# Split weights decoded from float64: three bitwise VectorE instructions behind a ScalarE scaling, and the low part made by an adding transfer

## The chip, the cores and the metric

The kernel runs on one core of a Trainium2 chip. The metric is the device time of one execution in microseconds (us); the median of three runs of the kernel before is 1067.02 us.

## The reference

Linear attention with random features, and behind it a two-layer feed-forward network whose activation is `h - tanh(h)`. There are 4608 tokens (8 batches of 576), 8 heads of 64, 128 features, a model width of 512 and an inner width of 2048.

```python
def phi(x):                                  # x: q or k, scaled by D**-0.25
    h = einsum('bhsd,md->bhsm', x, omega) - sum(x*x)/2
    return exp(h - max(h)) / sqrt(m)
q_p, k_p = phi(q), phi(k)
kv, z = einsum('bhsm,bhsd->bhmd', k_p, v), sum(k_p, axis=2)
x = (q_p @ kv) / (q_p . z + 1e-6)            # (4608, 512) after a transpose
h = x @ w_in                                 # w_in  (512, 2048), float64
out = (h - tanh(h)) @ w_out                  # w_out (2048, 512), float64
```

The two weight matrices are float64. The chip multiplies float32 and the reduced float32r, so the kernel turns each weight into a sum of two float32r numbers, a high and a low part, and multiplies with both.

## The kernel before, in words

**Weights.** The inner width is cut into 16 slices `f` of 128. One load, `fetch(f)`, brings slice `f` of both matrices as `raw[f]`: 128 partitions with 1024 float64 words, 1 MB. `decode(f)` makes `wt[f]` of it, which has the same size and lies in the same place: `wt[f][:, 0]` is the high part and `wt[f][:, 1]` the low part, 1024 numbers per partition each. The work tiles of a decode are `a` (the value being built, 4 KB per partition, two buffers) and `m` (the low bits, one buffer). ScalarE takes the absolute value of the upper half-words (L438) and copies a 16-bit piece from the middle of the words (L440). A clamp follows (L442), on VectorE for the first two slices and on GpSimd for the other 14. VectorE shifts and masks (L444), joins the sign (L445) and builds the low bits (L448). ScalarE rounds the result to the high part (L452, written `w<-a`), and VectorE isolates the exponent (L453) and multiplies the low bits by it (L454).

**Attention.** `k_unit(b, c)` handles batch `b` and head pair `c`: a load `kf`, features on TensorE into `pj`, exponentials on ScalarE (`phi_k`, L164), and the sums `pk`, from which `kvf` and `zb` are copied. GpSimd lays the last 64 tokens out in `kd` and `vd` (L184, L185). `q_unit(ch, c)` handles a chunk of 256 tokens: `qf`, `pj_q`, `phi_q`, denominators `dn` on VectorE (L347, L350), a scaling by them (L355 on ScalarE, L357 on VectorE), transposes `pt`, a copy `qt` (L369) and the product `pn` (L374). The quotient is split into `xh` and `xl`.

**Feed-forward.** Chunks 0 and 1 go through together, in 16 steps of one slice each: `h_0_s` is the first product (12 matmuls of 512 columns, L471), then tanh on ScalarE (`g`, L475), `g = h - g` on VectorE (L476), the rounding `gh` on ScalarE (L477), the rest `gl` on VectorE (L478), and 12 matmuls into four output banks (L489 to L491). There are two banks for `h`, so `h_0_2` starts when VectorE has read `h_0_0`. Chunks 2 to 17 follow, in eight steps of two slices each, with the later attention units between them; they use the weights that are on the chip by then.

**Order.** A Python generator per unit and a clock `t` set the program's order. The weights are decoded between attention units: slice `f` not before beat 4 + 2.5 `f`. A scheduler then orders each engine's instructions by its own estimate of time, and each engine carries its list out strictly in that order. Loads are issued by SyncE, in program order at first. The pool `a0` holds what only the first three chunks need; slices 10 to 15 take its place when it is closed, so their loads start only then.

Of the kernel before, what the change touches and what calls it, by code (L numbers as in the profile page):

```python
# [8 lines left out]
F32 = mybir.dt.float32  # L9
F32R = mybir.dt.float32r  # L10
U64 = mybir.dt.uint64
U32 = mybir.dt.uint32
U16 = mybir.dt.uint16
AF = mybir.ActivationFunctionType
ALU = mybir.AluOpType
AX = mybir.AxisListType
# [2 lines left out]
NT, DM, DFF = B * S, H * D, 2048  # L19
P = 128  # L20
# [5 lines left out]
E = D + 2  # L26
SCALE = float(D) ** -0.25
EPS = 1e-6 * M


@with_exitstack
def favor_attention_ffn(ctx: ExitStack, tc: tile.TileContext, qT, kT, va, vt, omT, w, out):
# [12 lines left out]
    nc = tc.nc  # L45
# [8 lines left out]
    def open_pool(name, side="right"):  # L54
        pools[name] = tc.tile_pool(name=name, bufs=1, side=side, reuse_waits="tile")
        return pools[name].__enter__()
# [7 lines left out]
    def bank(kind):  # L64
        tags = mode[kind]
        tags.append(tags.pop(0))
        return tags[-1]
# [26 lines left out]
    dec = open_pool("dec")  # L94
# [221 lines left out]
    def q_unit(ch, c):  # L316
# [23 lines left out]
        for h in range(2):  # L340
            for t in range(2):
                i = ix(h, t)
                for b, s, e in pieces:
                    s, e = max(s, t * P), min(e, (t + 1) * P)
                    if s < e:
                        r = slice(s - t * P, e - t * P)
                        nc.vector.tensor_tensor_reduce(  # L347
                            bank("junk")[r], ph[r, i], kvs[b, c][1][r, h], scale=1.0, scalar=EPS,
                            op0=ALU.mult, op1=ALU.add, accum_out=dn[r, i : i + 1])
# [63 lines left out]
    wt = {}  # L413

    raws = {}
# [11 lines left out]
    def decode(f):  # L427


        top = raws[f].bitcast(U32)[:, 1::2]  # L430
        topf = raws[f].bitcast(F32)[:, 1::2]
        mid = raws[f].bitcast(U16)[:, 1::4]
        a = dec.tile([P, 2 * DM], U32, tag="a", name=f"a{f}", bufs=2)
        m = dec.tile([P, 2 * DM], U32, tag="m", name=f"m{f}", bufs=1)

        nc.scalar.activation(a.bitcast(F32), topf, AF.Abs)  # L438

        nc.scalar.activation(m, mid, AF.Copy, scale=128.0)  # L440
        engine = nc.vector if f < 2 else nc.gpsimd
        engine.tensor_scalar(a.bitcast(F32), a.bitcast(F32), 2.0**-15, 122879.9921875,  # L442
                             op0=ALU.max, op1=ALU.min)
        nc.vector.tensor_scalar(a, a, 3, 0x3FFFF000, op0=ALU.logical_shift_left, op1=ALU.bitwise_and)  # L444
        nc.vector.scalar_tensor_tensor(out=a, in0=top, scalar=0xC0000000, in1=a,  # L445
                                       op0=ALU.bitwise_and, op1=ALU.bitwise_or)

        nc.vector.scalar_tensor_tensor(out=m, in0=top, scalar=23, in1=m,  # L448
                                       op0=ALU.logical_shift_left, op1=ALU.bitwise_or)

        wt[f] = places[f].tile([P, 2, 2 * DM], F32R, tag=f"w{f}", name=f"w{f}")
        nc.scalar.copy(wt[f][:, 0], a.bitcast(F32))  # L452
        nc.vector.tensor_scalar(a, a, 0xFF800000, None, op0=ALU.bitwise_and)  # L453
        nc.vector.scalar_tensor_tensor(out=wt[f][:, 1], in0=m, scalar=2.0**-43, in1=a.bitcast(F32),  # L454
                                       op0=ALU.mult, op1=ALU.mult)

    xh, xl = [sb.tile([P, 2, NC, TC], F32R, name=f"x{k}") for k in "hl"]

# [94 lines left out]
    while decoded < NF:  # L555
        if t in (2, 4):
            fetch(int(t == 4))
        if not gens and not start and len(places) < NF:
            close_pool("a0")
            weight_places(open_pool("w1", "left"), range(10, NF))  # L560
            for f in range(decoded, decoded + 2):
                fetch(f)
        if decoded in raws and t >= 4 + 2.5 * min(decoded, 16) + 2 * max(0, decoded - 16):
            decode(decoded)
            decoded += 1
            fetch(decoded + 2 - 1)
        if t == 15:
            mode.update(pj=["pj0", "pj1", "po1"], pk=["pk"], pt=["pt", "po0"])
        if done + 2 < decoded and t >= 23 + 1 * done:
            if done == 0:  # L570
                assert xdone[0] == xdone[1] == NC
                out_tiles(0, ("po0", "po1", "pj1", "pt"))
                mode.update(pj=["pj0"], pk=["pk"], pt=["pk"])
            step(done)
            done += 1
        tick(start.pop(t, ()))
        t += 1
# [89 lines left out]
```

## Time and profile before

| what | value |
|---|---|
| median of 3 runs | 1067.02 us (1065.73 to 1067.55) |
| profiled execution, from the first to the last instruction | 1065.4 us; no time of its own is given beside this span, and the median lies 1.6 us above it |
| TensorE busy | 1041.8 us, 98% |
| VectorE busy | 855.5 us, 80% |
| ScalarE busy | 696.4 us, 65% |
| GpSimd busy | 325.9 us, 31% |
| granted TensorE clock, mean | 0.998 |

The shares are means over the whole execution. Decoding lies in its first 160 us alone, where the engines stand otherwise than in the mean; a view of that stretch says more than the table. A row of the form `L440 ACT ACTIVATE m<-raw ... x16 | 18.7, 1166 | 9.7 <-DVE w L454` reads: line 440, ScalarE, what it writes and reads, 16 instructions of 1166 ns on average, and 9.7 us in which the engine was idle ahead of them, waiting for VectorE's L454.

### The profile page before, as it was taken

To read this page: it belongs to the slowest core of one execution; us is meant where nothing else is said; L and a number is where in the kernel's file an instruction comes from. 1 tells how busy PE (TensorE), PEld (TensorE's weight loads), DVE (VectorE), ACT (ScalarE), POOL (GpSimd) and SP (SyncE) were. 2 spreads that over 40 slices of the span, in tenths; PEclk is the share of its full clock that TensorE was granted. 3 is DMA by queue.
4 is the path that set the end of the run, shared out by engine and by line. 5 is a ranking of instruction groups with operands and counts; after the bars stand their busy time and mean duration, and the time that the engine had idled before them with its cause. 6 is when DMAs were issued, how large, how long until landed. Compare 5 with 4: busy or idle time off the path is not lost.

```text
span 1065.4 us, 20130 instructions
## 1 busy us (share of the span) xinstructions
PE 1041.8 (98%) x6760; PEld 945.6 (89%) x6760; DVE 855.5 (80%) x2910; ACT 696.4 (65%) x1773; POOL 325.9 (31%) x553
## 2 busy tenths in 40 slices
PE   7988999999999999999999999999999999999998
PEld 7766888999889999999999998999999999999997
DVE  5999995889998886789889878998888887666522
ACT  6997655777677665577777766677767675555422
POOL 4634541344333420133333344333333331000000
PEclk9999999999999999999999999999999999999999
DMA  8750401111111110011111111111101110000000
GB/s 265 237 213 3 187 1 42 53 39 46 31 53 33 54 33 31 11 53 33 53 34 53 34 37 44 33 53 29 47 25 49 33 37 11 30 16 21 1 21 21
DMA packets 35528, 55.90 MB, mean 52 GB/s; under 512 B 12256, under 2 KB 21600, under 8 KB 33376
## 3 DMA queue, kind: packets, MB, share of 16 engines
q1 hardware_dynamic: 35344, 54.57, 16.3%
q8 instruction: 54, 0.88, 0.3%
q14 instruction: 50, 0.41, 0.1%
q10 hardware_dynamic: 80, 0.03, 0.0%
HBM read 45.15 MB, written 9.44 MB: 51 GB/s over the span
## 4 chain that ended last, share of the span: by engine, by line
PE 61%; DVE 2%; ACT 1%; POOL 1%; issue 0%; DVEq 0%; POOLq 0%
PE h L471 26%; PE po L489 8%; PE po L490 8%; PE po L491 8%; PE pj_q L142 2%; PE pk L266 2%; PE pt L366 2%; PE pn L397 1%; PE pn L396 1%; PE pj_kb L142 1%; PE pj_ka L142 1%; PE pk L304 0%; PE pk L302 0%; DVE junk L347 0%; POOL khl L250 0%
## 5 line engine op out<-in xcount | busy, mean ns | idle before, releaser
L471 PE MATMUL h<-xh,w 128*128 128x256 f32 (+1 forms) x2176 | 450.1, 290 | 3.9 <-DVE g L476 2.1
L471 PEld LDWEIGHTS h<-xh,w 128*128 128x128 f32 x2176 | 354.8, 190 | 14.7 <-DVE g L476 3.2
L471 PE MATMUL h<-xl,w 128*128 128x256 f32 (+1 forms) x1088 | 315.8, 290 | 0.0
L489 PE MATMUL po<-w,gh 128*128 128x512 f32 x544 | 213.7, 393 | 0.0
L490 PE MATMUL po<-w,gh 128*128 128x512 f32 x544 | 213.3, 392 | 0.0
L471 PEld LDWEIGHTS h<-xl,w 128*128 128x128 f32 x1088 | 206.9, 190 | 6.0
L491 PE MATMUL po<-w,gl 128*128 128x512 f32 x544 | 209.2, 391 | 0.0
L477 ACT CAST gh<-g 128x512 fp32r<-128x512 f32 x144 | 89.4, 621 | 92.8 <-DVE g L476 91.3
L475 ACT ACTIVATE g<-h 128x512 f32<-128x512 f32 x144 | 85.4, 593 | 95.0 <-PE h L471 82.7
L476 DVE TENSOR_TENSOR g<-h,g 128x512 f32<-128x512 f32 x144 | 98.7, 686 | 57.8 <-ACT g L475 56.6
L478 DVE TENSOR_TENSOR gl<-g,gh 128x512 fp32r<-128x512 f32 x144 | 108.2, 751 | 34.9 <-ACT gh L477 33.1
L491 PEld LDWEIGHTS po<-w,gl 128*128 128x128 f32 x544 | 102.1, 188 | 20.5
L489 PEld LDWEIGHTS po<-w,gh 128*128 128x128 f32 x544 | 102.5, 188 | 16.2
L490 PEld LDWEIGHTS po<-w,gh 128*128 128x128 f32 x544 | 102.5, 188 | 15.3
L347 DVE CUSTOM_DVE_ANT_0 junk<-phi_q,zb 128x128 f32<-128x128 f32 (+1 forms) x320 | 98.5, 309 | 14.4 <-ACT phi_q L150 0.5
L150 ACT ACTIVATE phi_q<-phi_q,nb_q 128x128 f32<-128x128 f32 x240 | 79.6, 392 | 6.8 <-DVE nb_q L146 6.7
L442 POOL TENSOR_SCALAR a<-a 128x1024 f32<-128x1024 f32 x14 | 58.7, 4194 | 54.6 <-ACT a L438 37.2
L250 POOL TENSOR_TENSOR khl<-phi_ka,khl 128x256 fp32r<-128x256 f32 x48 | 37.9, 796 | 121.6 <-DVE khl L249 92.5
L258 POOL CAST vhl<-v 128x128 fp32r<-128x128 f32 (+1 forms) x144 | 45.8, 319 | 91.9 <-PE pk L266 71.5
L390 DVE TENSOR_TENSOR ql<-pt,qh 128x512 fp32r<-128x512 f32 x60 | 41.1, 685 | 32.3 <-ACT qh L389 31.8
L146 DVE CUSTOM_DVE_ANT_0 phi_q<-pj_q,phi_q 128x128 f32<-128x128 f32 x240 | 56.0, 283 | 2.3 <-ACT phi_q L143 2.2
L389 ACT CAST qh<-pt 128x512 fp32r<-128x512 f32 x60 | 34.9, 581 | 32.9 <-PE pt L366 32.6
(152 smaller groups left out, 1938.2 us busy)
## 6 DMA issues: line engine op xcount, KB each, us to landing
raw<-w SPq DMA_DIRECT2D x16, 1024.0 KB, 7.3
kf<-kT SPq DMA_DIRECT2D x32, 288.0 KB, 2.9
qf<-qT SPq DMA_DIRECT2D x72, 128.0 KB, 2.1
out<-o SPq DMA_DIRECT2D x36, 256.0 KB, 2.0
v<-vt SPq DMA_DIRECT2D x24, 288.0 KB, 2.8
v<-va SPq DMA_DIRECT2D x8, 288.0 KB, 5.9
omf<-omT ACTq DMA_DIRECT2D x1, 32.0 KB, 2.2
omf<-omT SPq DMA_DIRECT2D x1, 32.0 KB, 2.4
```

The costliest lines, as they stand in the source:

```text
L146: nc.vector.tensor_tensor_reduce(ph[:, j], pj[:, i, :M], ph[:, j], scale=-SCALE, scalar=3.0e38, op0=ALU.add, op1=ALU.min, accum_out=nb[:, ...
L150: nc.scalar.activation(ph[:, j], ph[:, j], AF.Exp, bias=nb[:, j : j + 1], scale=-1.0)
L347: nc.vector.tensor_tensor_reduce(bank("junk")[r], ph[r, i], kvs[b, c][1][r, h], scale=1.0, scalar=EPS, op0=ALU.mult, op1=ALU.add, accum_ou ...
L442: engine.tensor_scalar(a.bitcast(F32), a.bitcast(F32), 2.0**-15, 122879.9921875, op0=ALU.max, op1=ALU.min)
L471: nc.tensor.matmul(o, w_, x, start=i == 0, stop=i == len(prods) - 1)
L475: nc.scalar.activation(g, p, AF.Tanh)
L476: nc.vector.tensor_sub(g, p, g)
L477: nc.scalar.copy(gh, g)
L478: nc.vector.tensor_sub(gl, g, gh.bitcast(F32))
L489: nc.tensor.matmul(po[t], h, wt[f][:, 0, DM:], start=first, stop=False)
L490: nc.tensor.matmul(po[t], h, wt[f][:, 1, DM:], start=False, stop=False)
L491: nc.tensor.matmul(po[t], l, wt[f][:, 0, DM:], start=False, stop=last)
```

## The change: what it does

`decode(f)` builds the whole float32 value first. ScalarE scales the upper half-words by 2**-112 (L435 of the changed kernel), the clamp becomes a symmetric one (L437), VectorE shifts left by 3 (L438), joins the upper three bits of the lower half-word (L439) and the sign (L441). ScalarE then writes the rounded high part (L445) and, with a second instruction, its negative into the place of the low part (L446). A transfer issued by GpSimd adds the full value to that (L447): full value minus high part is the low part. The tile `m` is gone, and `a` has three buffers.

```diff
-        top = raws[f].bitcast(U32)[:, 1::2]
+        low, top = (raws[f].bitcast(U32)[:, i::2] for i in range(2))
         topf = raws[f].bitcast(F32)[:, 1::2]
-        mid = raws[f].bitcast(U16)[:, 1::4]
-        a = dec.tile([P, 2 * DM], U32, tag="a", name=f"a{f}", bufs=2)
-        m = dec.tile([P, 2 * DM], U32, tag="m", name=f"m{f}", bufs=1)
-        nc.scalar.activation(a.bitcast(F32), topf, AF.Abs)
-        nc.scalar.activation(m, mid, AF.Copy, scale=128.0)
+        a = dec.tile([P, 2 * DM], U32, tag="a", name=f"a{f}", bufs=3)
+        af = a.bitcast(F32)
+        nc.scalar.activation(af, topf, AF.Copy, scale=2.0**-112)
         engine = nc.vector if f < 2 else nc.gpsimd
-        engine.tensor_scalar(a.bitcast(F32), a.bitcast(F32), 2.0**-15, 122879.9921875,
-                             op0=ALU.max, op1=ALU.min)
-        nc.vector.tensor_scalar(a, a, 3, 0x3FFFF000, op0=ALU.logical_shift_left, op1=ALU.bitwise_and)
-        nc.vector.scalar_tensor_tensor(out=a, in0=top, scalar=0xC0000000, in1=a,
+        engine.tensor_scalar(af, af, -TOP, TOP, op0=ALU.max, op1=ALU.min)
+        nc.vector.tensor_scalar(a, a, 3, None, op0=ALU.logical_shift_left)
+        nc.vector.scalar_tensor_tensor(out=a, in0=low, scalar=29, in1=a,
+                                       op0=ALU.logical_shift_right, op1=ALU.bitwise_or)
+        nc.vector.scalar_tensor_tensor(out=a, in0=top, scalar=0x80000000, in1=a,
                                        op0=ALU.bitwise_and, op1=ALU.bitwise_or)
-        nc.vector.scalar_tensor_tensor(out=m, in0=top, scalar=23, in1=m,
-                                       op0=ALU.logical_shift_left, op1=ALU.bitwise_or)
         wt[f] = places[f].tile([P, 2, 2 * DM], F32R, tag=f"w{f}", name=f"w{f}")
-        nc.scalar.copy(wt[f][:, 0], a.bitcast(F32))
-        nc.vector.tensor_scalar(a, a, 0xFF800000, None, op0=ALU.bitwise_and)
-        nc.vector.scalar_tensor_tensor(out=wt[f][:, 1], in0=m, scalar=2.0**-43, in1=a.bitcast(F32),
-                                       op0=ALU.mult, op1=ALU.mult)
+        nc.scalar.copy(wt[f][:, 0], af)
+        nc.scalar.activation(wt[f][:, 1], af, AF.Copy, scale=-1.0)
+        nc.gpsimd.dma_start(wt[f][:, 1], af, accum_op=ALU.add)
```

Since the scheduler orders by its own estimates, the change also moves instructions that it does not name. Behind the decoding, lines of the changed kernel have numbers that are 10 lower (L465 for the tanh of L475). SyncE's list of loads is the same in both. Three places follow; names end in the buffer's number.

ScalarE before, around the tanh of step 0 (`g_0_0`) and its rounding (`gh_0_0`):

```order
L440 ACTIVATE m6_976<-raw6_746 128x1024
L438 ACTIVATE a7_1072<-raw7_908 128x1024
L355 ACTIVATE phi_q2_1_935<-phi_q2_1_935,dn_2_1_945 128x128 x2
L218 COPY kvf13_117<-pk_1_3_961 128x64 x2
L381 COPY x2_0_927<-pn_2_0_922 128x256
L475 ACTIVATE g_0_0_1110<-h_0_0_1097 128x512
L452 CAST w6_983<-a6_975 128x1024
L355 ACTIVATE phi_q2_2_1008<-phi_q2_2_1008,dn_2_2_1018 128x128 x2
L369 COPY qt_2_1_971<-pt_2_1_966 128x512
L224 COPY zb_1_3_1032<-pk_1_3_961 128x256
L477 CAST gh_0_0_1111<-g_0_0_1110 128x512
```

The same place of the changed kernel:

```order
L369 COPY qt_2_0_872<-pt_2_0_867 128x512
L355 ACTIVATE phi_q2_2_994<-phi_q2_2_994,dn_2_2_1004 128x128 x2
L218 COPY kvf13_117<-pk_1_3_949 128x64 x2
L369 COPY qt_2_1_959<-pt_2_1_954 128x512
L381 COPY x2_0_915<-pn_2_0_910 128x256
L465 ACTIVATE g_0_0_1094<-h_0_0_1081 128x512
L224 COPY zb_1_3_1018<-pk_1_3_949 128x256
L369 COPY qt_2_2_1025<-pt_2_2_1020 128x512
L445 CAST w9_1225<-a9_1219 128x1024
L446 ACTIVATE w9_1225<-a9_1219 128x1024
L467 CAST gh_0_0_1095<-g_0_0_1094 128x512
```

Before, the tanh of step 0 stands behind the ScalarE work of 21 decode instructions (eight of L438, seven of L440, six of L452); now behind that of 28 (ten scalings, nine roundings, nine negatives), and behind `phi_q2_2` and `qt_2_1` as well. On VectorE it is 32 decode instructions ahead of step 0's L476 (L466 now) where it was 35, all ten of the first slices instead of about seven. The two ScalarE instructions of slice 9 now stand between the tanh and `gh_0_0`, where those of slice 6 stood.

GpSimd before, from the last layouts to the clamp of slice 9:

```order
L442 TENSOR_SCALAR a4_734<-a4_734 128x1024
L184 COPY kd1_126<-kf_1_3_799 64x64 x2
L185 COPY vd1_127<-v1_125 64x66 x2
L442 TENSOR_SCALAR a5_896<-a5_896 128x1024
L442 TENSOR_SCALAR a6_975<-a6_975 128x1024
L442 TENSOR_SCALAR a7_1072<-a7_1072 128x1024
L442 TENSOR_SCALAR a8_1127<-a8_1127 128x1024
L442 TENSOR_SCALAR a9_1237<-a9_1237 128x1024
```

The same place of the changed kernel, where `DMA w<-a` is the issue of the adding transfer:

```order
L437 TENSOR_SCALAR a5_886<-a5_886 128x1024
L184 COPY kd1_126<-kf_1_3_789 64x64 x2
L185 COPY vd1_127<-v1_125 64x66 x2
L447 DMA w4_732<-a4_726 128x1024
L447 DMA w5_892<-a5_886 128x1024
L437 TENSOR_SCALAR a6_963<-a6_963 128x1024
L437 TENSOR_SCALAR a7_1058<-a7_1058 128x1024
L437 TENSOR_SCALAR a8_1111<-a8_1111 128x1024
L447 DMA w6_969<-a6_963 128x1024
L447 DMA w7_1064<-a7_1058 128x1024
L437 TENSOR_SCALAR a9_1219<-a9_1219 128x1024
```

Three clamps now run in a row ahead of the transfer of slice 6, and two issues stand ahead of the clamp of slice 9. The scaling of slice 9 on ScalarE writes the buffer of `a` that slice 6 used, so it waits until that transfer has landed.

TensorE before, at the end of step 2 (`h_0_2`) and behind it:

```order
L471 MATMUL h_0_2_1173<-xh_100,w2_447 128x512 x2
L471 MATMUL h_0_2_1173<-xl_101,w2_447 128x512
L471 MATMUL h_0_2_1173<-xh_100,w2_447 128x512
L374 MATMUL pn_2_1_1001<-qt_2_1_971,kvf01_107 128x64 x2
L374 MATMUL pn_2_1_1001<-qt_2_1_971,kvf11_115 128x192 x2
L366 MATMUL pt_2_2_1034<-ident_64,phi_q2_2_1008 128x128 x4
L489 MATMUL po1_0_1094<-w0_219,gh_0_0_1111 128x512
```

The changed kernel at the beginning of its step 2:

```order
L221 MATMUL pk_1_3_949<-ident_64,z_1_3_980 128x128 x2
L366 MATMUL pt_2_2_1020<-ident_64,phi_q2_2_994 128x128 x4
L374 MATMUL pn_2_1_987<-qt_2_1_959,kvf01_107 128x64 x2
L374 MATMUL pn_2_1_987<-qt_2_1_959,kvf11_115 128x192 x2
L461 MATMUL h_0_2_1155<-xh_100,w2_441 128x512
L461 MATMUL h_0_2_1155<-xl_101,w2_441 128x512
```

The transposes `pt_2_2` and the product `pn_2_1` stood behind `h_0_2` and stand ahead of it now; all other work ahead of `h_0_2` is the same.

2 lines of the change are left out of this document (1 added, 1 removed).

## The prediction

> **What bounds the kernel now.** Over the whole execution TensorE is busy 98% of the time. The change touches only the decoding, so the first view is the busy time by stretch, cut where the stretches differ (the columns are: length, then busy time and instructions of each engine):
>
> ```profile
> core 0: us, PE busy (x) PEld busy (x) DVE busy (x) ACT busy (x) POOL busy (x), PEclk, DMA share, GB/s
> 12.50:30.00 17.50, 14.15 (x78) 11.88 (x77) 15.03 (x29) 13.74 (x37) 8.46 (x9) 0.90 0.89 282
> 30.00:60.00 30.00, 28.11 (x161) 23.20 (x161) 30.00 (x91) 29.64 (x88) 13.57 (x19) 1.00 0.76 242
> 60.00:87.75 27.75, 21.95 (x118) 17.46 (x117) 27.39 (x102) 23.26 (x71) 8.97 (x3) 1.00 0.37 142
> 87.75:98.00 10.25, 8.12 (x47) 6.72 (x45) 10.02 (x22) 7.52 (x14) 7.79 (x2) 1.00 0.00 0
> 98.00:165.00 67.00, 67.00 (x299) 55.26 (x300) 59.66 (x75) 42.62 (x58) 31.35 (x10) 1.00 0.20 78
> ```
>
> From 98 us on TensorE is never idle, though six slices are still to be decoded: there a faster decode buys nothing. Between 30 and 87.75 us VectorE is full, and ScalarE nearly so: 0.36 us idle, then 4.49. TensorE idles 13.17 us in all from 12.5 to 98 us. That is everything the change could give back. Second view, what TensorE waited for from 20 to 98 us (the longest three):
>
> ```profile
> PE pn L374 <- ACT qt L369: 3.3, 4, 1.5
> PE pk L201 <- ACT phi_k L164: 2.5, 2, 2.0
> PE h L471 <- DVE g L476: 2.1, 2, 1.1
> ```
>
> It mostly waited for ScalarE; VectorE's two waits belong to steps 1 and 2. So ScalarE decides the stage, and the third view is ScalarE's own groups from 12.5 to 87.75 us, with what it waited for:
>
> ```profile
> L438 ACT ACTIVATE a<-raw 128x1024 f32<-128x1024 f32 x8 | 9.3, 1165 | 0.0
> L440 ACT ACTIVATE m<-raw 128x1024 uint32<-128x1024 uint16 x7 | 8.3, 1179 | 3.8 <-DVE w L454 3.8
> L355 ACT ACTIVATE phi_q<-phi_q,dn 128x128 f32<-128x128 f32 x20 | 7.8, 483 | 0.9 <-DVE dn L350 0.9
> L452 ACT CAST w<-a 128x1024 fp32r<-128x1024 f32 x6 | 6.6, 1101 | 0.1
> L214 ACT CAST kvw<-pk 128x128 fp32r<-128x128 f32 x4 | 1.4, 352 | 1.9 <-DVE z L210 1.9
> ```
>
> Of 8.61 us idle, VectorE caused 3.8 + 0.9 + 1.9 = 6.6 us.
>
> **What a decode costs.** VectorE's part by the rows of the first 200 us, and GpSimd's clamp:
>
> ```profile
> L448 DVE SCALAR_TENSOR_TENSOR m<-raw,m 128x1024 uint32<-128x1024 uint32 x16 | 20.4, 1272 | 0.1
> L445 DVE SCALAR_TENSOR_TENSOR a<-raw,a 128x1024 uint32<-128x1024 uint32 x16 | 20.3, 1269 | 0.0
> L454 DVE SCALAR_TENSOR_TENSOR w<-m,a 128x1024 fp32r<-128x1024 uint32 x16 | 19.5, 1217 | 0.1
> L453 DVE TENSOR_SCALAR a<-a 128x1024 uint32<-128x1024 uint32 x16 | 11.3, 703 | 4.1 <-ACT w L452 4.1
> L444 DVE TENSOR_SCALAR a<-a 128x1024 uint32<-128x1024 uint32 x16 | 11.0, 688 | 0.1
> L442 POOL TENSOR_SCALAR a<-a 128x1024 f32<-128x1024 f32 x14 | 58.7, 4194 | 54.6 <-ACT a L438 37.2
> ```
>
> VectorE: 0.688 + 1.269 + 1.272 + 0.703 + 1.217 = 5.15 us a slice before. Now one shift (0.688, at most L453's 0.703) and two joins of L445's shape (1.269 to 1.272): 3.23 us. It saves 1.92 us a slice, 30.7 us in all, 11.5 of them (six slices) behind 98 us, where TensorE covers them. ScalarE: 1.165 + 1.179 + 1.101 before. The scaling has the shape of L438. The negative has the shape of L452; its cost lies between 1.10 and L438's 1.17, and I take L452's, since shape and types are equal. That is 3.37 against 3.45: nothing gained worth counting. The clamp stays at 4.19 us.
>
> **What is added.** Sixteen issues on GpSimd and 16 transfers of 512 KB from SBUF to SBUF. Nearest rows, sizes with landing time, and an issue on SyncE's queue:
>
> ```profile
> raw<-w SPq DMA_DIRECT2D x16, 1024.0 KB, 7.3
> kf<-kT SPq DMA_DIRECT2D x32, 288.0 KB, 2.9
> 44.57 0.43 SPq L81 DMA_DIRECT2D raw<-w  x1
> ```
>
> An issue costs from 0.43 us (SyncE's) to 4.2 us (a clamp over the whole tile); I take 1.0 us, near the lower end because no elements pass through GpSimd. Sixteen are 16 us of GpSimd time; GpSimd idles 35 us between 30 and 87.75 us and 36 us from 98 to 165 us. Landing: between `kf` and `raw` a line gives 2.9 + (512 - 288) / 736 x 4.4 = 4.24 us; the ends are 2.9 us, `kf`'s own, and, since the target is read as well, 8.5 us, twice the line. I take 4.24. The Trainium skill ("DMA: Bandwidth & Descriptors", Anatomy of one DMA) fits a transfer issued from GpSimd by 2.0 us plus bytes over 436 GB/s; an estimate from that page is 3.2 us, and with it the wait of step 3 below, 0.5 us, would be gone and the sum 1066.3 us. The loads lose some of their engines' time (share 0.76 between 30 and 60 us); no TensorE wait of note ends on a load there, so I count nothing, and put its failure into the last rival.
>
> **The path that sets the end.** The relief goes to VectorE, but the order spends it: ahead of the tanh of step 0 stand ten slices' bitwise work instead of about seven, 32 decode instructions against 35, so VectorE is still full. ScalarE has 28 decode instructions there against 21. Its own rows around that tanh, and TensorE's around steps 2 and 3:
>
> ```profile
> 84.62 1.14 ACT L440 ACTIVATE m<-raw 128x1024 uint32<-128x1024 uint16 x1 [1.40 <-DVE w L454]
> 85.66 1.13 ACT L438 ACTIVATE a<-raw 128x1024 f32<-128x1024 f32 x1
> ...
> 87.75 0.59 ACT L475 ACTIVATE g<-h 128x512 f32<-128x512 f32 x1
> 88.23 1.04 ACT L452 CAST w<-a 128x1024 fp32r<-128x1024 f32 x1
> 89.17 0.70 ACT L355 ACTIVATE phi_q<-phi_q,dn 128x128 f32<-128x128 f32 x2
> 89.76 0.58 ACT L369 COPY qt<-pt 128x512 f32<-128x512 f32 x1
> 90.23 0.38 ACT L224 COPY zb<-pk 128x256 f32<-128x256 f32 x1
> 90.49 0.64 ACT L477 CAST gh<-g 128x512 fp32r<-128x512 f32 x1
> ```
>
> ```profile
> 89.82 0.50 PE L471 MATMUL h<-xh,w 128*128 128x512 f32 x1 [1.06 <-DVE g L476]
> ...
> 92.68 1.26 PE L374 MATMUL pn<-qt,kvf 128*128 128x64 f32 x8
> 93.78 0.60 PE L366 MATMUL pt<-ident,phi_q 128*128 128x128 f32 x4
> 94.14 0.47 PE L489 MATMUL po<-w,gh 128*128 128x512 f32 x1
> ...
> 97.93 0.50 PE L471 MATMUL h<-xh,w 128*128 128x512 f32 x1 [1.07 <-DVE g L476]
> ```
>
> From start to start a decode instruction takes 1.04 us (84.62 to 85.66) or 0.94 (88.23 to 89.17). The sum, step by step:
>
> 1. Seven more of them, at 1.04: +7.3 us. The two L355 of `phi_q2_2` (89.17 to 89.76) and the copy `qt_2_1` (89.76 to 90.23): +1.1 us.
> 2. All 6.6 us that ScalarE waited for VectorE come back: -6.6 us. The 2.0 us left wait for TensorE or stand at the start.
> 3. A new wait. The scaling of slice 9 must see the transfer of slice 6 landed. From the start of slice 6's scaling GpSimd needs 1.1 us until it may begin, three clamps in a row (12.6), an issue (1.0) and the landing (4.24): 18.9 us. ScalarE's list between the two scalings is seven decode instructions (three at 1.04, four at 0.94: 6.9 us) and 43 short ones. Those went at 0.267 us each from 30 to 60 us (29.64 us less eight decode instructions at 1.04, over 80), so 11.5 us, together 18.4. +0.5 us. What queues behind it is all of step 0.
>
> The tanh of step 0 starts at 87.75 + 7.3 + 1.1 - 6.6 + 0.5 = 90.05 us. `h_0_2` followed it by 2.07 us before, so it starts at 92.1 us now.
>
> 4. What that is worth on TensorE: `h_0_2` started at 89.82 us, lost another 1.07 at step 3 and was never idle again. The changed list has `pn_2_1` (92.68 to 93.78) and `pt_2_2` (93.78 to 94.14) ahead of `h_0_2`, 1.46 us of work that is then done. The kernel is even if `h_0_2` starts at 89.82 + 1.07 + 1.46 = 92.35 us. It starts 0.25 us ahead of that.
> 5. `gh_0_0` stands behind `zb`, `qt` and slice 9's pair: tanh 0.48, 0.26, 0.47, twice 0.94, rounding 0.5, together 3.6 us, and the pair itself is late: clamp 4.19 and VectorE 3.23 are 7.42 us, while ScalarE has 6.7 us of work between scaling and pair: 0.8 us. `gh_0_0` is there at 94.45 us; TensorE asks for it behind step 2's 12 matmuls (89.82 to 92.68 before: 2.86 us), at 94.96 or later. No cost.
> 6. Slices 10 to 15: three clamps, three issues, twice over, are 31 us of GpSimd in a stretch of 67 us, and a transfer may land some 3 us late before a rounding `gh` holds TensorE. Nothing, as long as landing stays near 4 us.
>
> Together -0.25 us. The span of the profiled execution is 1065.4 us; what lies around it is not in the trace, and the median lies 1.6 us higher. The changed span would be 1065.15 us; taken from the median, the 0.25 leave 1066.8 us. Anything within 0.2% (2.1 us) is what a measurement of this kernel can hardly tell from no change, so the forecast is: the same.
>
> **Rivals.**
>
> *ScalarE runs without a gap* (faster). If ScalarE also loses the 2.0 us and never waits for slice 6's transfer, the tanh starts at 87.75 + 8.4 - 8.6 = 87.55 us, and with VectorE prompt (tanh 0.48, subtraction 0.68, and little more) `h_0_2` 1.3 us later, at 88.85: 3.5 us under even, 1063.5 us. For it: 3.8 of the 6.6 us hung on the one buffer of `m`, which is gone. Against it: VectorE stays full. It becomes "faster" once `h_0_2` starts before 90.25 us.
>
> *The adding transfer lands late* (slower). At 8.5 us the scaling of slice 9 waits 4.3 us longer, and with it the tanh, `h_0_2` and the pair of slice 9: -0.25 + 4.3 gives 1071.1 us. It decides from a landing of 6.6 us (2.35 later than taken, for 2.1 above even). For it: the target is read and written, and the loads share the engines. Against it: no HBM is in the path.
>
> *GpSimd's issues are dear* (slower). At 4.2 us each, the landing of slice 6 is 3.2 us later, which gives 1070 us. Slices 10 to 15 then are 50 us of GpSimd (six clamps, six issues) and the last of them some microseconds late: up to 1075 us. It decides from 3.4 us an issue. Two rows speak for GpSimd being held up beside a full VectorE, the same pair of copies twice:
>
> ```profile
> 21.88 2.27 POOL L185 COPY vd<-v 64x66 f32<-64x66 f32 x2
> 39.04 0.55 POOL L185 COPY vd<-v 64x66 f32<-64x66 f32 x2
> ```
>
> The Trainium skill ("SBUF — State Buffer", Who interferes with whom) says that a VectorE instruction in a two-port mode locks GpSimd out of its port and so starves the writing of descriptors. The two rows agree that GpSimd can be held up by more than a microsecond. By that rule an issue waits for one VectorE tensor-scalar at most, 0.70 us by the rows above; the one issue that counts in step 3 would make the sum 1067.5 us. Loads that the transfers' traffic makes late I count with this case.
>
> **Chances.** The same 0.41 (the forecast; its own range is 1064.9 to 1069.1 us). ScalarE without a gap 0.20, and 0.02 more for a gain I don't see: faster 0.22. Landing late 0.27, dear issues or late loads 0.10: slower 0.37. The range runs from the first rival's end, 1063.5 us, over the second's 1071.1 with room for a late buffer at slices 13 to 15, to 1074 us; what is left out is most of the third rival and a larger gain.
>
> **What the profile after would show.** Right: VectorE's decode groups at 3.2 us a slice with the last at 1.27 us; ScalarE with almost no wait for VectorE before the tanh of step 0, and that tanh between 89 and 92 us; TensorE without idle time from about 93 us. Wrong: a ScalarE wait for a transfer ahead of the scalings, longer than 3 us; an issue on GpSimd of more than 2 us; or a tanh of step 0 ahead of 88 us, which would mean that ScalarE's list was not the bound.

## The result, and the profile after

| kernel | median us (runs) | ratio to the kernel before, 95% interval |
|---|---|---|
| before | 1067.28 (1065.73 to 1068.20) | |
| after | 1073.31 (1070.64 to 1075.56) | 1.0058 [1.0039, 1.0077] |

The change makes the kernel 0.6% slower, 6.0 us. The forecast was no change, at 1066.8 us. The profiled execution of the changed kernel took 1075.56 us, the longest of its four and 2.3 us above their median; its span is 1073.8 us, 8.4 us longer than the span before. The waits below are those of this execution.

First view, busy time by stretch, cut as before:

```profile
core 0: us, PE busy (x) PEld busy (x) DVE busy (x) ACT busy (x) POOL busy (x), PEclk, DMA share, GB/s
12.50:30.00 17.50, 13.38 (x73) 10.76 (x73) 14.78 (x32) 15.32 (x43) 9.95 (x11) 0.94 1.05 334
30.00:60.00 30.00, 27.63 (x141) 23.57 (x140) 27.71 (x95) 26.98 (x77) 18.47 (x19) 0.86 0.88 226
60.00:87.75 27.75, 23.93 (x118) 19.48 (x116) 25.59 (x76) 24.47 (x69) 16.82 (x11) 0.88 0.78 240
87.75:98.00 10.25, 3.49 (x15) 3.08 (x14) 5.28 (x21) 5.90 (x13) 4.48 (x2) 0.74 0.55 115
98.00:165.00 67.00, 67.00 (x308) 56.02 (x308) 42.06 (x60) 40.31 (x59) 29.23 (x15) 0.99 0.51 137
```

From 98 us on TensorE is never idle, as before, so the loss lies ahead of that, but for the last 1.6 us of a stretch at half clock. The fourth row is new: from 87.75 to 98 us no engine is busy for more than 58% of the time, TensorE idles 6.76 us (2.13 before), and yet the DMA engines are busy 55% of the time (0% before). The clock column is new too: 0.86, 0.88 and 0.74 where the granted clock had been 1.00. What TensorE waited for longest from 20 to 165 us, and ScalarE from 20 to 100 us (line, releaser, us in total, times, longest):

```profile
PE h L461 <- DVE kvw L215: 6.8, 1, 6.8
PE pt L366 <- DVE xl L410: 3.6, 4, 1.8
```

```profile
ACT a L435 <- issue: 5.2, 1, 5.2
ACT qt L369 <- PE pt L366: 3.0, 2, 2.1
ACT x L381 <- PE pn L374: 1.5, 1, 1.5
ACT a L435 <- ACT phi_q L164: 0.9, 1, 0.9
ACT a L435 <- DMA w<-a: 0.9, 1, 0.9
ACT g L465 <- PE h L461: 0.5, 1, 0.5
```

No ScalarE wait for the decode's VectorE work is left. In its place stands one wait of 5.2 us ahead of a scaling (L435). ScalarE's rows around it, and the two issues of GpSimd that belong to it:

```profile
83.98 1.41 ACT L164 ACTIVATE phi_q<-pj_q,nb_q 128x128 f32<-128x128 f32 x4
90.56 1.12 ACT L435 ACTIVATE a<-raw 128x1024 f32<-128x1024 f32 x1 [5.17 <-issue]
91.58 1.04 ACT L445 CAST w<-a 128x1024 fp32r<-128x1024 f32 x1
92.51 1.06 ACT L446 ACTIVATE w<-a 128x1024 fp32r<-128x1024 f32 x1
...
94.20 0.38 ACT L409 CAST xh<-pn 128x256 fp32r<-128x256 f32 x1
...
99.73 0.60 ACT L465 ACTIVATE g<-h 128x512 f32<-128x512 f32 x1 [0.48 <-PE h L461]
```

```profile
79.92 0.90 POOL L447 DMA_DIRECT2D w<-a  x1
82.86 0.85 POOL L447 DMA_DIRECT2D w<-a  x1 [2.05 <-ACT phi_q L164]
DMA to landing us min/median/max: 4.5/5.2/10.6
```

The scaling at 90.56 us is slice 9's; it writes into the buffer from which slice 6's transfer reads. That transfer was issued at 79.92 us and had the longest landing, 10.6 us: 79.92 + 10.6 = 90.5 us, where the wait ends. (The row says "issue", since the profile shows no releaser; the experiments below test it. Slice 9's own weight load is not what the scaling waited for: it was issued at 76.48 us and had landed 5.2 us later, at 81.6 us.) Queued behind it are slice 8's pair (91.58, 92.51) and the `xh` of the last head pair (94.20), without which `h_0_0` can't be finished; TensorE therefore stands still for 6.8 us. SyncE issued three 1 MB weight loads just then, the tenth to twelfth of the sixteen (by the program's order those of slices 9, 10 and 11, so the loads of slices 10 and 11 start here already, ahead of the last work in `a0`; before the change the same three went out from 68.46 us on):

```profile
76.48 3.65 SPq L81 DMA_DIRECT2D raw<-w  x3
```

### The profile page after: what moved, and what is told of

The parts are those of the page before. It is cut to its first block, busy times and chain, and to the rows that moved or that the text cites. A ratio compares the mean times of both kernels' runs of the same rounds, so it can differ in the third digit from the quotient of the medians.

```text
span 1073.8 us, 20182 instructions
## 1 busy us (share of the span) xinstructions
PE 1047.1 (98%) x6760; PEld 952.0 (89%) x6760; DVE 832.3 (78%) x2878; ACT 694.3 (65%) x1773; POOL 335.2 (31%) x569
## 4 chain that ended last, share of the span: by engine, by line
PE 61%; DVE 2%; ACT 1%; POOL 1%; issue 0%; DVEq 0%; POOLq 0%
PE h L461 26%; PE po L479 8%; PE po L480 8%; PE po L481 8%; PE pj_q L142 2%; PE pk L266 2%; PE pt L366 2%; PE pn L397 1%; PE pn L396 1%; PE pj_kb L142 1%; PE pj_ka L142 1%; PE pk L304 0%; PE pk L302 0%; POOL khl L250 0%; DVE junk L347 0%
## 5 line engine op out<-in xcount | busy, mean ns | idle before, releaser
L466 DVE TENSOR_TENSOR g<-h,g 128x512 f32<-128x512 f32 x144 | 98.8, 686 | 69.0 <-ACT g L465 67.9
L465 ACT ACTIVATE g<-h 128x512 f32<-128x512 f32 x144 | 85.4, 593 | 100.3 <-PE h L461 90.8
L437 POOL TENSOR_SCALAR a<-a 128x1024 f32<-128x1024 f32 x14 | 52.5, 3769 | 32.2 <-ACT a L435 25.9
```

What stands on the lines that cost most here:

```text
L437: engine.tensor_scalar(af, af, -TOP, TOP, op0=ALU.max, op1=ALU.min)
L465: nc.scalar.activation(g, p, AF.Tanh)
L466: nc.vector.tensor_sub(g, p, g)
```

## Experiments

Where two kernels are compared, it is by their ratio to the kernel before on the same chip. "Tanh" is the start of step 0's tanh in the profiled execution: 87.75 us before, 99.73 us after.

### 1. Transfer, buffers, subtraction

**Plain copy**: the same order of instructions, without the adding.

```diff
-        nc.gpsimd.dma_start(wt[f][:, 1], af, accum_op=ALU.add)
+        nc.gpsimd.dma_start(wt[f][:, 1], af)
```

> Edit: the transfer writes instead of adding (the low part becomes the full value, so the addition is left out); every engine's order is word for word that of the changed kernel. Theory A (the 10.6 us landing of slice 6's transfer comes from sharing the DMA engines with three weight loads): it still lands in 8 us or more, ScalarE still stands 3 to 5 us ahead of slice 9's scaling, about 1072 us. Theory B (the adding itself, which reads its target, is what takes long): median landing falls from 5.2 to 3 us or less, slice 6's under 6 us, no stall, 1066 to 1068 us. Theory C (slice 9's own weight load, not the transfer, holds the scaling): stall 5 us and 1073 us as before.

1071.52 us, 1.0039 [1.0024, 1.0054]. The wait ahead of slice 9's scaling shrank to 2.3 us, the tanh came at 95.32 us. Copies landed in

```profile
DMA to landing us min/median/max: 2.9/3.2/8.6
```

So the adding alone takes 2.0 us of landing at the median, and less landing means less wait; an issue took less too, 0.59 us at the median against 0.89. Slice 6's copy went out at 79.52 us and landed after 7.4 us, at 87.0 us, and slice 9's scaling started at 87.03 us: it is the transfer that it waits for. The times lie between what the theories gave. So the adding is a part of the loss at most, not all of it; the intervals of the two kernels overlap.

**Four buffers for `a`** (`bufs=4`).

> Edit: four buffers of the tile a, so that slice 9's scaling waits for the transfer of slice 5, not of slice 6. The order shifts a little: 30 decode instructions ahead of the tanh of step 0 (28 in the changed kernel). Theories A and B (the wait for the transfer costs the time): no ScalarE stall over 1 us ahead of slice 9's scaling, no TensorE wait of 6.8 us, 1066 to 1069 us. Theory C (the weight load): the stall of about 5 us stays, 1072 to 1074 us. Theory D (28 instructions of decoding ahead of step 0 are the cost, whatever they wait for): 2 more of them, 1073 us or above.

1074.99 us, 1.0070 [1.0055, 1.0085]. The wait is gone, the tanh comes at 98.15 us all the same: the scheduler used the fourth buffer to put 30 decode instructions ahead of it instead of 28, and ScalarE was full:

```profile
60.00:87.75 27.75, 17.82 (x91) 13.96 (x91) 27.27 (x83) 27.75 (x78) 18.47 (x9) 0.95 0.80 231
```

**Transfers left out.**

> Edit: the transfers are gone (the addition is left out); scaling, clamp, three bitwise instructions, rounding and negative stay. 28 decode instructions stand ahead of the tanh of step 0 as in the changed kernel. Theories A and B: the tanh of step 0 starts near 90 us, as the prediction's sum had it, and the kernel takes 1065 to 1067.5 us. Theory D (the order itself costs the time): 1070 us or more.

1074.78 us, 1.0067 [1.0052, 1.0082]. The tanh comes at 91.58 us, close to the forecast's 90.05, but the list is another one: `pn_2_1` and `pt_2_2` no longer stand ahead of `h_0_2`, and TensorE lost 2.34 us at 120 to 165 us, where it had lost none. An edit that lets the scheduler order anew is no clean test here.

**Low part by a subtraction on VectorE**, without negative and transfer.

```diff
-        nc.scalar.activation(wt[f][:, 1], af, AF.Copy, scale=-1.0)
-        nc.gpsimd.dma_start(wt[f][:, 1], af, accum_op=ALU.add)
+        nc.vector.tensor_sub(wt[f][:, 1], af, wt[f][:, 0].bitcast(F32))
```

> Edit: low part = full value minus high part by one VectorE subtraction, in place of the negative and the adding transfer. ScalarE has 20 decode instructions ahead of the tanh of step 0 (28 in the changed kernel, 21 before), VectorE 42 (32 and 35). Theory A: faster than before, since neither ScalarE's extra work nor the landing is there: 1063 to 1066 us. Rival: VectorE, full from 30 to 88 us, is the bound and its 42 instructions (about 44 us against 37) put step 0 off: 1068 to 1072 us.

1078.64 us, 1.0099 [1.0083, 1.0116]; VectorE is the bound, 27.75 of 27.75 us from 60 to 87.75 us, and the tanh comes at 102.88 us.

### 2. Is it the number of slices decoded ahead?

My theory by then was that ScalarE pays for the slices that the scheduler now decodes further ahead (28 instructions against 21). The pace sets that number and leaves the other instructions ahead of the tanh as they are.

```diff
-        if decoded in raws and t >= 4 + 2.5 * min(decoded, 16) + 2 * max(0, decoded - 16):
+        if decoded in raws and t >= 4 + 4 * min(decoded, 16) + 2 * max(0, decoded - 16):
```

> The change with one number altered: slice f may be decoded from unit 4 + 4f on instead of 4 + 2.5f, so that 21 of ScalarE's decode instructions stand ahead of step 0's tanh, as before the change, instead of 28; the other work ahead of it stays (192 instructions). Theory D (the scheduler spends VectorE's relief on decoding further ahead, and ScalarE pays for it): seven instructions of about 1.08 us leave ScalarE ahead of step 0, 7.6 us, and with them the scaling of slice 9 and its 5.2 us of waiting for slice 6's transfer; the tanh comes at 87 to 92 us instead of 99.7, and the time is 1061 to 1066 us. Theory T (the transfers and the weight loads beside them are what delays, wherever the decode stands): some other scaling waits as long, the tanh comes after 95 us, the time stays at 1070 to 1074. Theory L (the slices left behind are missed in the feedforward steps): the tanh comes early, but the time stays above 1067, with TensorE waiting for w after 100 us.

1080.59 us, 1.0119 [1.0100, 1.0139].

> As the run with pace 4, but 4 + 3.5f: 24 decode instructions of ScalarE ahead of step 0's tanh, the same other work. Theory D: between the change (28) and pace 4 (21), some 3 to 4 us of tanh later than pace 4, 1064 to 1069 us. Theory T: 1070 to 1074. Theory L: below pace 4, since fewer slices are left behind.

1077.46 us, 1.0096 [1.0078, 1.0114].

> Pace 4 with a plain copy in place of the adding transfer (the low part is then the whole value, not the remainder): the same order of instructions as pace 4, but transfers that landed in 3.2 us at the median instead of 5.2. Theory D: at pace 4 no scaling waits for a transfer, so the two take the same time within 1.5 us. Theory T: the plain copy is faster by 2 us or more, as it was at pace 2.5 (1071.5 against 1073.3).

1072.75 us, 1.0059 [1.0040, 1.0078].

The last edit of the pace releases one slice per step once the steps run: `t >= min(4 + 4 * decoded, 22 + decoded)`.

> The change with slice f decoded from unit 4 + 4f on, but from 22 + f where that is earlier: 21 decode instructions of ScalarE ahead of step 0's tanh as in the run with pace 4, where the tanh came at 90.4 us and the feedforward steps then lost 5.2 us at 120 to 165 us and 3.5 us at 165 to 300 us for want of slices; here one slice is released per step. Theory L (the loss at pace 4 is late slices alone): the tanh comes at 88 to 92 us and TensorE is busy all through 120 to 165 us: 1062 to 1068 us. Theory W (a slice not decoded ahead of step 0 is missed later, however the rest is paced): idle time of 3 us or more stays in 120 to 300 us, 1070 or more.

1079.05 us, 1.0110 [1.0094, 1.0125]. The pace of 3.5 lies between. At pace 4 the tanh came at 90.37 us, as theory D had it, and the kernel was slower than ever. The run with the cap shows where it went:

```profile
120.00:165.00 45.00, 39.85 (x170) 31.05 (x168) 32.42 (x36) 27.58 (x34) 29.29 (x15) 1.00 0.42 79
165.00:300.00 135.00, 129.49 (x826) 116.26 (x825) 107.68 (x386) 89.76 (x233) 46.84 (x88) 0.99 0.18 50
```

TensorE idles 5.15 and 5.51 us, 0 and 1.57 us in the changed kernel. A slice that isn't decoded ahead of step 0 is missed later; the early tanh is worth nothing then. Theory D fell: decoding ahead was no mistake of the scheduler. These runs also say that the cost of the transfers isn't the same everywhere: at pace 4 the plain copy is 7.8 us faster, where theory D wanted less than 1.5.

**Two buffers for `a`**, as before the change, lead to the same place.

> The change with two buffers for a, as before the change, instead of three: 22 decode instructions of ScalarE ahead of step 0's tanh (21 before the change, 28 with three buffers), 26 of VectorE (35 before). Each scaling then waits for the transfer of the slice before the last. Theory A: tanh of step 0 at 88 to 92 us, 1064 to 1068 us. Theory W: tanh early, but TensorE idle for 3 to 6 us at 120 to 165 us for want of slices, 1072 to 1080, as with pace 4.

1092.72 us, 1.0255 [1.0239, 1.0271]. With 22 decode instructions ahead the tanh still comes at 94.78 us only, since the scalings now wait for transfers all the way (from 20 to 165 us):

```profile
ACT a L435 <- DMA w<-a: 9.8, 4, 5.2
ACT a L435 <- issue: 4.8, 1, 4.8
```

The third buffer is worth some 20 us to the changed kernel: each `a` is held until its transfer has landed.

### 3. The wait alone, and the clock alone

**Loads one slice earlier**, to take them away from slice 6's transfer.

```diff
-            for f in range(decoded, decoded + 2):
+            for f in range(decoded, decoded + 3):
...
-            fetch(decoded + 2 - 1)
+            fetch(decoded + 2)
```

(and one `fetch(2)` at the start).

> The change with every weight slice loaded one slice earlier, so that other loads stand beside slice 6's transfer. Theory T (three 1 MB weight loads beside the transfer of slice 6 make it land after 10.6 us and ScalarE wait 5.2): another transfer is hit or none; if none, the stall goes and the time is 1067 to 1069 us. Theory D: 30 decode instructions stand ahead of step 0's tanh instead of 28, so the time stays at 1072 to 1076 even where no transfer lands late.

1075.25 us, 1.0079 [1.0062, 1.0096], tanh at 99.52 us. The long wait is gone here too, but 30 decode instructions stand ahead: as with four buffers, it doesn't separate the two. What the run does show is what makes a transfer late. Slice 5's was issued 0.6 us behind a weight load now (64.74 us), slice 6's with none under way (73.02 us), and they landed after

```profile
w<-a POOLq DMA_DIRECT2D x1, 512.0 KB, 9.4
w<-a POOLq DMA_DIRECT2D x1, 512.0 KB, 4.8
```

where the changed kernel had 5.7 and 10.6 us. The changed kernel's own sixteen agree: the four that ran beside a weight load for 5 us or more (slices 0, 3, 6 and 7) landed after 8.7 to 10.6 us, the nine with none under way after 4.5 to 5.2 us.

**A buffer for slice 9's `a` alone.** Now the lists stay as they are, but for that scaling.

```diff
-        a = dec.tile([P, 2 * DM], U32, tag="a", name=f"a{f}", bufs=3)
+        a = dec.tile([P, 2 * DM], U32, tag="a9" if f == 9 else "a", name=f"a{f}", bufs=1 if f == 9 else 3)
```

> The change with one buffer more, for slice 9's a alone, so that its scaling on ScalarE need not wait for slice 6's transfer. Apart from that scaling, which stands one place earlier, and four places behind the tanh of step 0, the lists of instructions are those of the change (20 lines of difference on ScalarE). Theory S (the loss is the 5.2 us that ScalarE stands still there, and what follows from it, TensorE idle for 6.8 us and then at half its clock): the tanh of step 0 comes at 92 to 95 us instead of 99.7, TensorE keeps its full clock at 90 to 100 us, 1066 to 1069 us. Theory H (TensorE's granted clock falls to half wherever the engines in front of it feed it too thinly, and most of the loss is work done at half clock, in three episodes of 6.8 to 10.2 us): the third episode goes, the first two (28 and 69 us) stay, 1068 to 1071 us. Theory A (ScalarE's 28 decode instructions alone): no better than 1071.

1069.30 us over 11 runs, 1.0028 [1.0016, 1.0039]: 3.2 us less than the change by the ratios, 4.0 us by the medians. (The two profiled executions lie 8.0 us apart: one is the longest of four, the other the second shortest of eleven.) The stretch that had stood still:

```profile
87.75:98.00 10.25, 9.19 (x53) 7.94 (x54) 8.06 (x26) 8.56 (x23) 2.22 (x2) 1.00 0.49 92
91.76 0.60 ACT L465 ACTIVATE g<-h 128x512 f32<-128x512 f32 x1
```

**Small matmuls issued twice**, to keep TensorE's clock up. In the changed kernel the clock fell to half for 10.2 us at 28 us, and again at 69 and 93 us. One of the added edits:

```diff
-        for h in range(2):
+        for h in [0, 1] * (2 if n in ('0_2',) else 1):
             nc.tensor.transpose(pk[:, 256 + 128 * h : 384 + 128 * h],
```

> The change with four small matmuls issued twice, each before or at the start of its sum, so that results stay as they are: two transposes of z of unit 0_2, one matmul of pj_q1_0 and the first of pk_0_3. They lie at 24 to 28 us, where TensorE was busy 42 to 45% of 3.4 us before its granted clock fell to half for 10.2 us; they bring that to some 57%. ScalarE's, GpSimd's and the loads' lists are unchanged. Theory H: the first episode goes or gets shorter, and TensorE, which was busy all through it, does 3 to 5 us of work more by 40 us; the time falls by 1 to 4 us, to 1069 to 1072. Theory S or A: the clock of the first 40 us makes no difference to the end, since the other engines set the pace then: 1072 to 1075.

1075.83 us, 1.0077 [1.0065, 1.0090]. The edit did what it should: the same 10 us, in the change and here, are

```profile
28.00:38.20 10.20, 9.78 (x34) 8.54 (x35) 8.09 (x21) 7.18 (x20) 8.46 (x12) 0.50 0.86 229
```

```profile
28.00:38.00 10.00, 6.95 (x42) 5.53 (x40) 9.88 (x31) 8.33 (x24) 7.58 (x9) 1.00 1.06 280
```

with 42 matmul records instead of 34 in 6.95 us of work instead of 9.78; TensorE went idle instead (3 us), because the other engines set the pace there. Half clock came back later, for 3.4 us at 38.8 us, and the wait for slice 6's transfer stayed. ScalarE's 2.1 us of waiting for `pt` at 38 us went, and another wait of 2.4 us for a buffer came (7.5 us in two waits, one of them the 5.1 already known; lines here are one higher):

```profile
ACT a L436 <- issue: 7.5, 2, 5.1
```

No gain.

> Both: slice 9's own buffer, the four matmuls issued twice, and the two transposes of z of unit 1_0 (at 62 us, ahead of the second episode). Theory H: no or one short episode at half clock, 1063 to 1067 us, as fast as the kernel before or faster. Theory S: as slice 9's own buffer alone, within 1 us. Theory A: 1071 or more.

1069.88 us, 1.0031 [1.0019, 1.0042], as slice 9's own buffer alone, and 4.9 us less than the repeated matmuls without that buffer by the ratios, with intervals well apart. Theory H fell for the stretch up to 80 us: with the repeated matmuls alone half clock there had shrunk from 17.0 to 6.8 us, for no gain.

**Plain copies with slice 9's own buffer.**

> Slice 9's own buffer with plain copies in place of the adding transfers (the low part is then the whole value), the same order. Theory T (the adding transfers' use of the DMA engines, 28% of them in the first 100 us, delays loads on which the rest of the loss rests): faster than with adding by 1.5 us or more. Otherwise the same within 1 us, 1068.5 to 1070.

1067.83 us over 11 runs, 1.0009 [1.0000, 1.0017], some 2 us faster than with adding (the intervals meet at 1.0016 to 1.0017), in the same order and with no scaling waiting long for a transfer in either. Its profiled execution spent 13.6 us at half clock,

```profile
62.00:75.60 13.60, 11.87 (x43) 10.16 (x44) 11.63 (x33) 12.84 (x33) 11.29 (x4) 0.50 0.34 134
```

and was the shortest profiled one of all changed kernels, 1066.98 us: half clock that early cost nothing to be seen.

**Slice 9's scaling behind step 0**, with its own buffer: slices from 7 on are released two beats later.

> Slice 9's own buffer, and slices from 7 on released two beats later, which takes slice 9's scaling to the place behind step 0 (27 decode instructions ahead of its tanh instead of 28) and leaves the rest of ScalarE's list ahead of it as it was. Theory A (ScalarE's extra decode instructions are what is left of the loss): 1 us less than slice 9's own buffer, 1067.5 to 1069. Theory W (what isn't decoded ahead is missed in the feedforward steps): 1070 to 1076, with TensorE idle at 120 to 165 us.

1068.82 us over 11 runs, 1.0012 [1.0003, 1.0021]: of the loss only 1.3 us is left. This is the best version that still computes everything; none beat the kernel before.

### 4. The same wait removed in another way

**Slice 6 alone by subtraction**, so that slice 9 has no transfer to wait for and no buffer is added.

> The change, but slice 6's low part comes from a subtraction on VectorE, without negative and transfer, so that slice 9's scaling has no transfer to wait for and no buffer is added; one ScalarE instruction fewer stands ahead of step 0, one VectorE instruction more. Theory S (ScalarE's wait for slice 6's transfer is the larger part of the loss): no stall of 5 us at 85 to 90 us, tanh of step 0 at 90 to 94 us, 1066 to 1070 us as with slice 9's own buffer. Theory B (that gain came from the buffer, which also moved a late weight load): 1072 or more.

1073.20 us, 1.0058 [1.0044, 1.0072]: no gain, though the wait is gone and the tanh comes at 93.94 us. Its profiled execution was at half clock for 10.2 us at the start of the steps:

```profile
85.50:88.50 3.00, 0.04 (x1) 0.00 (x0) 2.87 (x17) 2.20 (x4) 1.83 (x1) 1.00 0.24 44
90.00:100.20 10.20, 9.35 (x31) 7.69 (x30) 6.30 (x21) 6.77 (x14) 0.86 (x1) 0.50 0.37 71
```

The first row shows TensorE idle for 3 us, the second the half clock behind it. I filled the gap, with four transposes issued four times.

> The run without slice 6's transfer, with the four transposes of pt_2_0 issued four times over (1.8 us of TensorE, ahead of its idle 3.1 us at 85.5 to 88.7 us, results unchanged, ScalarE's list the same but for seven lines). Theory H2 (half clock costs time where TensorE is the bound, from some 88 us on, and not before): TensorE's busy share of 3.4 us at 86 to 90 us rises from 8 to 38% to 50% or more, the 10.2 us at half clock at 90 to 100 us go or shrink to 3.4, and the time falls from 1073.2 by 2 to 4 us, to 1069 to 1071. Otherwise (the order of the instructions alone): 1072.5 to 1074.5.

1073.17 us, 1.0072 [1.0054, 1.0089]. The clock stayed up, and the time as it was:

```profile
90.00:100.20 10.20, 6.77 (x41) 5.52 (x40) 9.31 (x42) 8.61 (x19) 2.32 (x3) 1.00 0.27 51
```

So it isn't the clock here either. The subtraction is one more instruction for VectorE, and ScalarE waits for VectorE again, 4.0 us ahead of the tanh, the first time for a reduction right behind the subtraction (rows of the run without the filling):

```profile
78.29 1.14 ACT L164 ACTIVATE phi_q<-pj_q,nb_q 128x128 f32<-128x128 f32 x4 [1.56 <-DVE nb_q L162]
...
86.34 1.05 ACT L445 CAST w<-a 128x1024 fp32r<-128x1024 f32 x1 [0.80 <-DVE a L441]
...
91.81 0.69 ACT L355 ACTIVATE phi_q<-phi_q,dn 128x128 f32<-128x128 f32 x2 [1.64 <-DVE dn L350]
```

With slice 9's own buffer that was 1.7 us. The list around the tanh differs too: the tanh stands ahead of the copy `qt_2_1` here, and TensorE waits for that copy with the product `pn_2_1`, which stands ahead of `h_0_2`:

```profile
95.65 2.50 PE L374 MATMUL pn<-qt,kvf 128*128 128x64 f32 x8 [0.67 <-ACT qt L369]
```

So `h_0_2` follows the tanh by 4.7 us here and by 4.2 us with the filling, by 1.9 us with slice 9's own buffer. No run changes one of the two alone.

### What the runs say together

Six kernels have the change's list, but for slice 9's three instructions, some small repeated matmuls or the kind of transfer. Their profiled executions:

| kernel | tanh of step 0, us | span, us | difference |
|---|---|---|---|
| plain copy, slice 9's own buffer | 91.23 | 1065.2 | 974.0 |
| slice 9's own buffer | 91.76 | 1065.8 | 974.0 |
| the same with repeated matmuls | 92.95 | 1067.4 | 974.5 |
| plain copy | 95.32 | 1070.1 | 974.8 |
| the change | 99.73 | 1073.8 | 974.1 |
| the change with repeated matmuls | 100.39 | 1074.4 | 974.0 |

With one list, the span is the tanh plus 974 us, within 0.8 us. The kernel before has another list (tanh at 87.75 us, span 977.7 us longer, step 1's tanh 6.0 us behind); with the changed list its span of 1065.4 us is met by a tanh at 91.3 us. So the loss of the profiled execution is what makes the tanh 8.4 us later than that, and nothing behind it.

The start of `h_0_2` ties other lists in as well. With slice 9's own buffer, with the subtraction for slice 6 and in the change it is

```profile
93.65 0.53 PE L461 MATMUL h<-xh,w 128*128 128x512 f32 x1
98.65 0.78 PE L464 MATMUL h<-xh,w 128*128 128x512 f32 x1
101.62 0.53 PE L461 MATMUL h<-xh,w 128*128 128x512 f32 x1
```

and the span is 972.2, 972.7 and 972.2 us longer. In the six above, both kernels with the subtraction for slice 6, the one with all subtractions, the one with earlier loads and the one with slice 9's scaling behind step 0 it is 972.0 to 972.7 us, in the kernel before 975.6 us. The whole difference between these eleven lies ahead of `h_0_2`, that of the subtraction for slice 6 included.

## Why the prediction was wrong, point by point

1. *Seven more decode instructions and 1.1 us of short ones*: right in kind. They stand ahead and nothing covers them; the profile's means are 1.205 (L435), 1.140 (L445) and 1.155 us (L446), 3.50 us a slice where I had 3.37. VectorE's part was 0.845 + 1.256 + 1.241 = 3.34 us by the means of L438, L439 and L441, where I had 3.23.
2. *All 6.6 us of waits for VectorE come back, and 2.0 us stay*: the first half was right, the second was mis-sized. Beside the long wait ScalarE waited 3.0 + 1.5 + 0.9 + 0.9 + 0.5 = 6.8 us, 4.8 more than the 2.0. Of these 5.0 us end on TensorE, nearly all of them in stretches at half clock (28 to 38.2 us, 92.8 to 99.6 us):

```profile
38.02 0.59 ACT L369 COPY qt<-pt 128x512 f32<-128x512 f32 x1 [2.12 <-PE pt L366]
...
96.80 0.59 ACT L369 COPY qt<-pt 128x512 f32<-128x512 f32 x1 [0.93 <-PE pt L366]
98.88 0.37 ACT L381 COPY x<-pn 128x256 f32<-128x256 f32 x1 [1.49 <-PE pn L374]
```

   The same eight matmuls of `pn_2_0` took 2.34 us there and 1.36 us in the run with slice 9's own buffer:

```profile
96.50 2.34 PE L374 MATMUL pn<-qt,kvf 128*128 128x64 f32 x8
```

```profile
89.91 1.36 PE L374 MATMUL pn<-qt,kvf 128*128 128x64 f32 x8
```

   The later three waits follow from the stall, which left TensorE idle; a falling clock was nowhere in my sum.
3. *The new wait, +0.5 us*: **the step that failed**, by the size of its landing. The mechanism was named right: slice 9's scaling, slice 6's transfer, the third buffer, all of step 0 queued behind. The issue was right (0.90 us, 1.0 taken). GpSimd's clamps were shorter than taken (3.77 us against 4.19). The landing was wrong: 4.24 us taken between loads from HBM, 5.2 us at the median of the 16, and 10.6 us for the one that counts, which went out right behind the last of three 1 MB loads; it lies above my upper end of 8.5 us. The wait was 5.17 us, where I had 0.5: 4.7 us too little. It is the sign of being wrong that I had named, a ScalarE wait for a transfer of more than 3 us.
4. Steps 2 and 3 make 4.8 + 4.7 = 9.5 us, and the tanh came 99.73 - 90.05 = 9.68 us later than forecast. `h_0_2` was due at 92.1 us, even at 92.35, and started at 101.62: 9.3 us late, for 8.4 us of span. The even point was 0.9 us too early: behind `h_0_2` the kernel before takes 3.4 us more than the changed one (975.6 against 972.2), and I had counted 1.07 + 1.46 = 2.53. I don't know what the 0.9 us are; that they went my way was luck.
5. *`gh_0_0` and slices 10 to 15 cost nothing*: right. TensorE is busy for all 67 us from 98 to 165 us.

The rival that lands late had the right place and the right sign; at its 8.5 us it gave 1071.1 us, against 1073.3 measured. I had taken the line between two medians for a transfer that runs beside weight loads; those loads themselves had landed after 5.1 to 11.3 us before the change, 7.3 being their median. The row that would have warned me was the first view's own DMA share: 0.89, 0.76 and 0.37 before the change, to which sixteen transfers of 512 KB and their adding come. The rival of dear issues is excluded by the 0.85 to 1.03 us that an issue took; its two rows had told little, since VectorE was full beside the quick pair of copies too (0.56 of 0.56 us, 2.17 of 2.27 beside the slow one).

Shown by runs: the wait for slice 6's transfer is the larger part of the loss of 6 us, 3.2 us by the ratios and 4.0 by the medians (its buffer alone, same lists; the two intervals touch at 1.0039), 4.9 us in the pair with repeated matmuls (1.0077 to 1.0031, intervals apart). Shown too, by the run with earlier loads, is that weight loads beside it make a transfer late. Less sure: the adding is some 2 us more even where no scaling waits long (1.0028 to 1.0009, 1.0058 to 1.0039 with the wait); in each of these two pairs the intervals overlap, and only at pace 4 are they apart. One scaling less ahead of step 0 gives back perhaps another 0.5 to 1.7 us (1069.30 to 1068.82 us, 1.0028 to 1.0012; the intervals overlap). Not settled: through which wait the adding still costs 2 us where no scaling hangs on it, and which of VectorE's waits and the moved copy `qt` takes the gain from the subtraction for slice 6.

## What to carry to other kernels

A transfer that reads a work buffer lengthens that buffer's life by its landing time, so price the wait of the instruction that takes the buffer next, and price the landing by the busiest stretch it can fall into, not by a median. Where a scheduler orders by its own estimates, test a wait with an edit that leaves the lists as they are (one buffer for one slice): four broader edits removed the same wait and hid the answer behind a new order. Work decoded ahead isn't waste because it delays the first step; holding it back cost 5.2 us and 3.9 us of TensorE later.

## What the runs showed of the hardware that I had not expected

- An adding transfer of 512 KB from SBUF to SBUF landed in 5.2 us at the median, a plain copy in 3.2 us; the slowest adding one in 10.6 us, the slowest copy in 8.6 us. What made them slow were loads beside them: adding transfers of the changed kernel took 4.5 to 5.2 us with no weight load under way and 8.7 to 10.6 us beside one. The Trainium skill ("DMA: Bandwidth & Descriptors", Anatomy of one DMA) gave an estimate of 3.2 us; the plain copy agrees with it, the adding one doesn't.
- TensorE's granted clock fell to half in each of the profiled executions, in stretches of 3.4, 6.8, 10.2 or (once) 13.6 us, within 0.2 us. It needed no idle window: in the changed kernel TensorE had been busy 45% of 3.4 us ahead of the drop at 28 us, in gaps of 1.0 us and less, and it stayed at half for 10.2 us though it was busy for 9.78 of them:

```profile
24.60:28.00 3.40, 1.54 (x6) 0.97 (x6) 3.33 (x15) 3.40 (x9) 3.40 (x1) 0.99 1.12 265
```

  The Trainium skill ("TensorE: Matmul & The Clock Gate", Part 1) has a window of about 3.4 us, and one idle window drops the clock there, one busy window restores it. The lengths bear the window out; the rest isn't always so: here the drop came behind a window busy 45%, and it took three windows with 9.78 us of work in 10.2 to restore the clock.
- Taking half clock away ahead of the steps gained nothing (28 us), nor did 13.6 us of it from 62 to 75.6 us cost anything that shows in the end: ScalarE and VectorE set the pace there. What it costs behind a stall, at 93 to 100 us of the changed kernel, no run separates from the stall.
